# Transposing bf16 pairs as 4-byte elements in a fused attention and maxout FFN kernel, with PSUM copies re-split and the issue order redone

## The chip, the cores and the metric

One core of one Trainium2 chip runs the whole program. The metric is device time in microseconds (us), median of several executions. "Span" is the time from the first to the last instruction in a trace; it is some 1.8 us shorter than the device time. PE is TensorE (PEld its weight loads), DVE is VectorE, ACT is ScalarE, POOL is GpSimd. PSUM is the memory into which this kernel's matmuls write and from which its copies on DVE or ACT (L153, L155) read. "Clock" is the TensorE clock that was granted, as a share of full speed. Unless a run is called slow, only fast runs are compared.

## The reference, cut to what matters

```python
# q, k, v: [8, 8, 576, 64]   phi: [8, 8, 576, 32]
a = softmax(phi, axis=2)                       # over the sequence
k_m = einsum('bhsm,bhsd->bhmd', a, k)          # 32 memory slots per head
v_m = einsum('bhsm,bhsd->bhmd', a, v)
attn = softmax(q @ k_m^T / 8, axis=-1)         # over the 32 slots
x = (attn @ v_m), heads side by side           # [4608, 512]
out = max(x @ w1, x @ w2, x @ w3) @ w_out
```

A remark on what "correct" means here. The scores are so small that the output hardly depends on q: with q set to zero the reference moves by 8e-7 of its norm. The comparison with the reference passes all kernels below, even one that reads wrong q on purpose (e8_step16), so it does not prove that the new layout is right. I checked the layout by separate arithmetic: transpose 32x32 blocks of pairs, contract even and odd columns in turn, compare with q times k_m. It agreed to 1e-14. That the chip moves the pairs as intended is shown by no run, since none of them can tell.

## The kernel before

Batch by batch, letters name pieces of work that a long text puts into an order. Each engine executes its share in that order (e10 below shows DVE idle for 2.33 us with ready work behind). The pieces that matter:

```python
accp = tile_pool(bufs=4, PSUM)     # four accumulators, shared by ALL matmul groups
EVAC = {"D": "aaaa", "T": "avvva"} # who copies block n out of PSUM: a = ACT, v = DVE

# B: att_kv: k_m, v_m (PE)     N: att_kv_norm (DVE): rden, kvn; kvn holds k_m in two halves
    in0=kvp[:, g, 0:D].rearrange("p (h d) -> p h d", h=2)...   # half h = columns 32h..32h+31
# K: att_kv_t: 3 PE transposes of kvn, one DVE copy -> kvt
# Q: att_q (two halves of the heads), 32x32 blocks on DVE
    qT = work.tile([P, NP, NC, 2, R], BF16)                    # R = 32
    nc.vector.transpose(out=qT[:, j]..., in_=q[:, j]...)       # 1152 bf16 per partition
# S: att_score: 32 matmuls of 32 x 288, contraction over half h
    rhs=qT[r, j, :, h, :], start=(h == 0), stop=(h == 1)
# M, R, X: softmax over the slots (PE sums, ACT ln and exp, DVE multiply)
# D0..D3: fold v_m into w1-w3, w2-w3 and w3*w_out (PE), copied out by EVAC["D"]
# F0..F11: first FFN product; even n: relu on ACT, odd n: max on DVE
# T0..T4: output tile, 8 matmuls of 512 columns, copied out by EVAC["T"], stored
# L0, L1, L2: load phi, k and v, q of a batch   Z: warm-up matmuls without use
for w in """ E@0 Z26@0 B@0 N@0 ... B@1 N@1 D3@0 K@1
    D2@1 L1@2 D0@1 Q0@1 Q1@1 T1@0 D1@1 S@1 T3@0 M0@1 ... """.split(): ...   # piece@batch
```

The softmax here doesn't subtract the row's maximum and nothing guards it: scores larger than these inputs give would overflow.

Of the kernel before, what the change touches and what calls it, by code (L numbers as in the profile page):

```python
# [8 lines left out]
FP32 = mybir.dt.float32  # L9
BF16 = mybir.dt.bfloat16  # L10
# [5 lines left out]
def kernel(  # L16
# [14 lines left out]
    B, H, S, D = q.shape  # L31
    M = phi.shape[-1]
    P = 128
    NP = H // 2
    NG = NP // 2
    HP = P // 2
    NC = S // HP
    R = 32
# [8 lines left out]
    work = ctx.enter_context(tc.tile_pool(name="work", bufs=2))  # L47
# [24 lines left out]
    loaded = {}  # L72
# [69 lines left out]
            )  # L142


    EVAC = {"D": "aaaa", "T": "avvva"}

    def evacuate(kind, n, out_, in_):
        e = EVAC[kind][n]
        if e == "s":
            nc.scalar.copy(out=out_[:, 0], in_=in_[:, 0])  # L150
            nc.vector.tensor_copy(out=out_[:, 1], in_=in_[:, 1])
        elif e == "a":
            nc.scalar.copy(out=out_, in_=in_)  # L153
        else:
            nc.vector.tensor_copy(out=out_, in_=in_)  # L155
# [69 lines left out]
    def att_kv_norm(b):  # L225

        s = st[b]
        kvp = s["kvp"]
        rden = work.tile([P, NG], FP32, name="rden")
        nc.vector.reciprocal(out=rden, in_=kvp[:, :, 2 * D])  # L230
        kvn = work.tile([P, 3, P], BF16, name="kvn")
        nc.vector.tensor_tensor(
            out=kvn[:, 0].rearrange("p (a d) -> p a d", a=NG),
            in0=kvp[:, :, D : 2 * D],
            in1=rden.unsqueeze(2).to_broadcast([P, NG, D]),
            op=ALU.mult,
        )
        for g in range(NG):
            kn = kvn[:, 1:3, HP * g : HP * (g + 1)]
            nc.vector.tensor_scalar_mul(  # L240
                out=kn.rearrange("p h (t d) -> p h t d", t=2),
                in0=kvp[:, g, 0:D]
                .rearrange("p (h d) -> p h d", h=2)
                .unsqueeze(2)
                .to_broadcast([P, 2, 2, R]),
                scalar1=rden[:, g : g + 1],
            )
        s["kvn"] = kvn
# [12 lines left out]
    def att_q(b, n):  # L261


        s = st.setdefault(b, {})
        if "qT" not in s:
            s["qT"] = work.tile([P, NP, NC, 2, R], BF16, name="qT")
        j = halves[n]
        nc.vector.transpose(  # L268
            out=s["qT"][:, j].rearrange("p j c h r -> p (j c h r)"),
            in_=loaded[b]["q"][:, j].rearrange("p j c d -> p (j c d)"),  # L270
        )

    attns = {}
# [1 line left out]
    def att_score(b):  # L275

        s = st[b]
        kvt, qT = s["kvt"], s["qT"]
        e2 = s["e2"] = work.tile([P, NG, S], BF16, name="e2")
        if b % 2 == 0:  # L280
            attns[b // 2] = work.tile([P, NG, 2 * S], BF16, name="attn")
        sc = [
            acc_pool.tile([P, 2, BANK], FP32, name="sc", tag="acc") for _ in range(NG)
        ]
        for h in range(2):
            for j in range(NP):
                for a in range(NG):
                    for t in range(2):
                        r = slice(R * (2 * a + t), R * (2 * a + t + 1))
                        nc.tensor.matmul(  # L290
                            sc[a][M * j : M * (j + 1), t, 0:SH],
                            lhsT=kvt[r, 1 + h, M * j : M * (j + 1)],
                            rhs=qT[r, j, :, h, :],
                            start=(h == 0),
                            stop=(h == 1),
                            tile_position=(R * (2 * a + t), M * j),
                        )
        for a in range(NG):
            nc.scalar.activation(  # L299
                out=e2[:, a].rearrange("p (t r c) -> p t r c", t=2, c=NC),  # L300
                in_=sc[a][:, :, 0:SH].rearrange("p t (c r) -> p t r c", c=NC),
                func=AF.Exp,
                scale=0.125,
            )
# [96 lines left out]
    def ffn2(b, t, last=False):  # L401


        hT, attn = hts[b // 2], attns[b // 2]
        c0 = S - HP if t == 4 else (b % 2) * (S + HP) + t * P
        if last:
            return ffn2_last(b, c0)
        po = acc_pool.tile([P, DM], FP32, name="po", tag="acc")
        for fc in range(FT):
            nc.tensor.matmul(  # L410
                po,
                lhsT=hT[:, fc, c0 : c0 + P],
                rhs=wo_sb[:, fc, :],
                start=(fc == 0),
                stop=False,
            )
        for g in range(NG):
            if t < 4:
                nc.tensor.matmul(  # L419
                    po,  # L420
                    lhsT=attn[:, g, c0 : c0 + P],
                    rhs=wp3s[b][:, g, :],
                    start=False,
                    stop=(g == NG - 1),
                )
            else:
                for u in range(2):
                    nc.tensor.matmul(  # L428
                        po[HP * u : HP * (u + 1)],
                        lhsT=attn[:, g, c0 + HP * u : c0 + HP * (u + 1)],  # L430
                        rhs=wp3s[b - 1 + u][:, g, :],
                        start=False,
                        stop=(g == NG - 1),
                        tile_position=(0, HP * u),
                    )
        ot = opool.tile([P, DM], FP32, name="ot")
        r0 = (b // 2) * 2 * S + c0
        rows = out[r0 : r0 + P, :]
        evacuate("T", t, ot, po)
        nc.sync.dma_start(out=rows, in_=ot)  # L440
# [40 lines left out]
    def issue(b, n):  # L481

        if not 0 <= b < B or (n == "T4" and b % 2 == 0):
            return
        i = int(n[1:]) if len(n) > 1 else None
        {
            "L": lambda: (load_ph, load_kv, load_q)[i](b),
            "E": lambda: [att_exp(b, h) for h in (halves if b == 0 else [slice(0, NP)])],
            "B": lambda: att_kv(b) if b else first_kv(),
            "N": lambda: att_kv_norm(b),  # L490
            "K": lambda: att_kv_t(b),
            "Q": lambda: att_q(b, i),
            "S": lambda: att_score(b),
            "M": lambda: att_sum(b, i),
            "R": lambda: att_rec(b, i),
            "X": lambda: att_mul(b, i),
            "D": lambda: fold(b, i),
            "F": lambda: ffn1(b, i),
            "T": lambda: ffn2(b, i),
            "W": lambda: w3_t(i),  # L500
            "O": lambda: w3_o(i),
            "V": lambda: w_diff(i),
            "Z": lambda: warm_up(i),
        }[n[0]]()

    def run(b, text):

        for w in text.split():
            issue(b + w.count("+") - w.count("-"), w.rstrip("+-"))

    for w in """
        E@0 Z26@0 B@0 N@0 Z5@0 K@0 Q0@0 Q1@0 Z15@0 S@0 Z6@0 M1@0 R1@0 W2@0 W0@0 W1@0 M0@0
        X1@0 Z4@0 O0@0 O1@0 V0@0 R0@0 X0@0 O2@0 Z3@0 D0@0 V1@0 O3@0 F2@0 F6@0 V2@0 L2@2 F0@0
        D1@0 F4@0 D2@0 F3@0 E@1 F1@0 F10@0 F7@0 L0@2 F11@0 F8@0 F9@0 F5@0 B@1 N@1 D3@0 K@1
        D2@1 L1@2 D0@1 Q0@1 Q1@1 T1@0 D1@1 S@1 T3@0 M0@1 L0@3 Q0@2 M1@1 R0@1 R1@1 X0@1 X1@1
        E@2 T0@0 T2@0 F8@1 Q1@2 F6@1 F7@1 F2@1 L2@3 F3@1 F9@1 F4@1 D3@1 B@2 F10@1 N@2 F5@1
        F0@1 K@2 E@3 F1@1 F11@1 Q1@3 S@2 T0@1 Q0@3 M0@2 R0@2 X0@2 M1@2 L1@3 L0@4 T4@1 R1@2
        L2@4 L1@4 T3@1 L0@5 X1@2 D0@2 D2@2 B@3 D1@2 N@3 T2@1 F2@2 K@3 F10@2 F3@2 F0@2 Q0@4
        S@3 F11@2 F8@2 F4@2 F1@2 M1@3 F9@2 R1@3 E@4 F5@2 Q1@4 M0@3 R0@3 T1@1 F6@2 F7@2 D3@2
        B@4 X1@3 D2@3 D0@3 T0@2 N@4 L0@6 X0@3 K@4 L2@5 F2@3 D1@3 S@4 T1@2 E@5 F3@3 F8@3 L1@5  # L520
        F9@3 F6@3 F4@3 F10@3 L0@7 M1@4 F5@3 E@6 T2@2 R1@4 M0@4 F0@3 Q1@5 R0@4 F7@3 T3@2 L1@6
        F1@3 L2@6 F11@3 D3@3 B@5 N@5 D0@4 D1@4 T0@3 X1@4 L1@7 K@5 T1@3 D3@4 Q0@5 D2@4 X0@4
        L2@7
    """.split():
        n, b = w.split("@")
        issue(int(b), n)
    for b in range(4, B - 1):
        run(b, "T4- D3+ S+ L2++++ T3- F2 F4 Q1++ F5 F10 F3 F0 F6 F1 F8 M1+ F11 F9")
        run(b, "L0+++++ F7 R1+ M0+ X1+ T2- R0+ D2+ B++ Q0++ D1+ N++ D0+ L1++++ T1 E+++")
        run(b, "K++ X0+ T0")  # L530
    run(B - 1, "F2 F10 F6 F3 F11 F0 T2- F1 F4 F8 F9 F7 F5 T3- T4 T4- T3 T2 T1")
    ffn2(B - 1, 0, last=True)


# [28 lines left out]
```

## Time and profile before

| | before |
|---|---|
| median of the first measurement | 173.88 us (173.47 to 174.13, 4 runs) |
| span of the trace | 171.7 us |
| PE, DVE, ACT busy | 161.2, 102.4, 107.5 us |
| batch 0's first fold starts; batch 1's kv matmuls start; PE ends | 27.45; 37.50; 168.0 us |
| gaps on PE after the first fold starts | 3.76 us |

The last row is the sum of the seven bracketed idle times that PE's timeline lists after its first fold (the prediction below shows them). That list leaves out idle times of some 0.1 us. It is the number to follow through this document.

The groups that the change touches, from the view of groups by shape. Columns: line, engine, operation, output and inputs, shapes, count; busy us and mean ns of one; idle before them and what ended it.

```profile
L153 ACT CAST wp<-wps 128x1024 bf16<-128x1024 f32 x32 | 31.3, 1017 | 10.3 <-PE wps L355 10.2
L268 DVE STREAM_TRANSPOSE qT<-qq 128x1152 bf16<-128x1152 bf16 x16 | 21.6, 1364 | 1.7 <-DMA qq<-in_q_dram 1.7
L155 DVE COPY ot<-po 128x512 f32<-128x512 f32 x24 | 16.6, 690 | 30.5 <-PE po L419 30.5
L153 ACT COPY ot<-po 128x512 f32<-128x512 f32 x11 | 6.4, 584 | 11.4 <-PE po L428 6.3 <-PE po L419 4.8
L290 PE MATMUL sc<-qT,kvt 32*32 32x288 bf16 x256 | 3.7, 286 | 0.0
```

The transposes take 21.6 us of DVE, a fifth of its busy time; all fold copies are on ACT.

### The profile page before, as it was taken

How to read it: one execution, taken by the hardware profiler on the slowest of the kernel's cores; microseconds unless marked ns; L12 is line 12 of the kernel's file. 1: busy time of each engine (PE TensorE's matmuls, PEld its weight loads, DVE VectorE, ACT ScalarE, POOL GpSimd, SP SyncE). 2: the span in 40 equal slices, each digit the busy share in tenths (PEclk: the TensorE clock that was granted, in tenths of full speed). 3: DMA queues.
4: the chain of work that ended last, by engine and by line, in shares of the span. 5: the costliest groups of instructions: out<-in, count | busy, mean ns of one | idle time of the engine just before them, and what ended most of it. 6: DMA issues, size and time to landing. Idle time of an engine off the chain costs nothing.

```text
span 171.7 us, 4491 instructions
## 1 busy us (share of the span) xinstructions
PE 161.2 (94%) x1925; PEld 91.5 (53%) x1948; DVE 102.4 (60%) x160; ACT 107.5 (63%) x154; POOL 28.3 (17%) x43
## 2 busy tenths in 40 slices
PE   7999999987999999899999997999999999999991
PEld 2354644552567546664755445654764475466350
DVE  6407346679588945795468546883787058337240
ACT  4100528946897877899996586886785777752100
POOL 7951111110515100051332110000000000000000
PEclk9999999999999999999999999999999999999998
DMA  5999999999999999999999999953103310221333
GB/s 157 162 202 211 206 211 274 211 207 266 222 314 262 216 298 260 237 244 258 230 247 290 232 258 244 224 131 124 65 0 107 141 65 4 112 75 61 119 126 124
DMA packets 21973, 31.76 MB, mean 185 GB/s; under 512 B 1216, under 2 KB 16576, under 8 KB 21952
## 3 DMA queue, kind: packets, MB, share of 16 engines
q0 software_dynamic: 16080, 21.43, 65.3%
q1 hardware_dynamic: 5728, 9.90, 16.5%
q8 instruction: 15, 0.25, 0.6%
q10 hardware_dynamic: 144, 0.13, 0.2%
q14 instruction: 6, 0.05, 0.1%
HBM read 39.32 MB, written 9.44 MB: 284 GB/s over the span
## 4 chain that ended last, share of the span: by engine, by line
PE 43%; DMA 41%; issue 6%; DVE 3%; POOL 3%; ACT 1%; POOLq 0%
DMA kvo<-in_v_dram 20%; PE po L410 16%; PE acc L380 15%; DMA ph<-in_phi_dram 11%; DMA qq<-in_q_dram 10%; PE po L419 5%; POOL kvo L96 3%; PE wps L355 2%; PE kvp L216 2%; DVE qT L268 2%; PE sm L311 1%; PE po L451 1%; PE po L428 1%; ACT e L205 1%; PE sc L290 0%
## 5 line engine op out<-in xcount | busy, mean ns | idle before, releaser
L380 PE MATMUL acc<-attn,wp 128*128 128x288 bf16 x384 | 51.2, 286 | 1.3 <-DVE hT L392 1.0
L410 PE MATMUL po<-wo_sb,hT 128*128 128x512 bf16 x191 | 50.1, 379 | 1.1
L380 PEld LDWEIGHTS <-wp 128*128 128x128 bf16 x384 | 37.0, 98 | 13.8 <-issue 1.9
L392 DVE TENSOR_TENSOR hT<-acc,h 128x576 bf16<-128x576 f32 x48 | 34.4, 749 | 12.6 <-PE acc L380 8.3
L153 ACT CAST wp<-wps 128x1024 bf16<-128x1024 f32 x32 | 31.3, 1017 | 10.3 <-PE wps L355 10.2
L390 ACT ACTIVATE h<-acc 128x576 bf16<-128x576 f32 x48 | 29.8, 652 | 11.2 <-PE acc L380 9.9
L155 DVE COPY ot<-po 128x512 f32<-128x512 f32 x24 | 16.6, 690 | 30.5 <-PE po L419 30.5
L410 PEld LDWEIGHTS <-hT 128*128 128x128 bf16 x210 | 19.4, 98 | 23.2 <-issue 4.4
L268 DVE STREAM_TRANSPOSE qT<-qq 128x1152 bf16<-128x1152 bf16 x16 | 21.6, 1364 | 1.7 <-DMA qq<-in_q_dram 1.7
L140 PE MATMUL po<-warm 128*128 128x512 bf16 x65 | 18.2, 428 | 1.5 <-DVE warm L128 1.2
L419 PE MATMUL po<-wp,attn 128*128 128x512 bf16 x62 | 18.4, 379 | 0.0
L299 ACT ACTIVATE e<-sc 128x576 bf16<-128x576 f32 x16 | 9.6, 661 | 10.7 <-PE sc L290 10.7
L153 ACT COPY ot<-po 128x512 f32<-128x512 f32 x11 | 6.4, 584 | 11.4 <-PE po L428 6.3
L335 DVE TENSOR_TENSOR attn<-e,r 128x576 bf16<-128x576 bf16 x16 | 11.9, 746 | 1.0 <-ACT r L330 1.0
L140 PEld LDWEIGHTS <-warm 128*128 128x128 bf16 x68 | 6.9, 108 | 10.3 <-issue 4.0
L205 ACT ACTIVATE e<-ph 128x1152 bf16<-128x1152 f32 (+1 forms) x9 | 9.6, 1064 | 4.5 <-DMA ph<-in_phi_dram 4.5
L324 ACT ACTIVATE ln<-sm 128x576 f32<-128x576 f32 x16 | 10.4, 649 | 1.7 <-PE sm L311 1.6
L89 POOL DMA_DIRECT2D ph<-in_phi_dram x7 | 5.3, 756 | 36.9 <-ACT e L205 33.4
L330 ACT ACTIVATE r<-ln 128x576 f32<-128x576 f32 x16 | 10.9, 683 | 0.5
L419 PEld LDWEIGHTS <-attn 128*128 128x128 bf16 x62 | 6.1, 98 | 7.3
L216 PE MATMUL kvp<-kvo,e 64*32 64x192 bf16 x576 | 8.3, 243 | 0.8 <-DMA kvo<-in_v_dram 0.8
L355 PE MATMUL wps<-w_sb,kvt 64*32 64x512 bf16 x192 | 8.3, 381 | 0.9 <-DVE kvt L258 0.5
(45 smaller groups left out, 100.8 us busy)
## 6 DMA issues: line engine op xcount, KB each, us to landing
out_dram<-ot SPq DMA_DIRECT2D x35, 256.0 KB, 4.1
qq<-in_q_dram POOLq DMA_DIRECT2D x8, 576.0 KB, 16.2
ph<-in_phi_dram POOLq DMA_DIRECT2D x7, 576.0 KB, 17.9
kvo<-in_k_dram POOLq DMA_DIRECT2D x7, 576.0 KB, 16.3
kvo<-in_v_dram POOLq DMA_DIRECT2D x7, 576.0 KB, 18.5
w_sb<-in_moe_w_dram POOLq DMA_DIRECT2D x3, 768.0 KB, 19.0
wo_sb<-in_moe_w_out_dram POOLq DMA_DIRECT2D x1, 768.0 KB, 16.7
ph<-in_phi_dram SPq DMA_DIRECT2D x2, 288.0 KB, 4.4
```

The source lines that it names most:

```text
L140: nc.tensor.matmul(po[:, 0:BANK], lhsT=warm[:, 0:P], rhs=warm, start=True, stop=True)
L153: nc.scalar.copy(out=out_, in_=in_)
L155: nc.vector.tensor_copy(out=out_, in_=in_)
L216: nc.tensor.matmul(kvp[M * j : M * (j + 1), a, 0 : 3 * D], lhsT=s["e"][r, j, c, :], rhs=kv[r, :, j, c, :], start=(c == 0), stop=(c == NC - 1),
L268: nc.vector.transpose(out=s["qT"][:, j].rearrange("p j c h r -> p (j c h r)"), in_=loaded[b]["q"][:, j].rearrange("p j c d -> p (j c d)"),)
L335: nc.vector.tensor_tensor(out=attns[b // 2][:, g, (b % 2) * S : (b % 2 + 1) * S], in0=s["e2"][:, g, 0:S], in1=s["r", g], op=ALU.mult,)
L355: nc.tensor.matmul(ps[M * j : M * (j + 1), a, :], lhsT=s["kvt"][r, 0, M * j : M * (j + 1)], rhs=w12[r, j, n * BANK : (n + 1) * BANK] if n ...
L380: nc.tensor.matmul(acc[:, h, 0:SH], lhsT=wps[b][:, g, w * DF + ft * P : w * DF + (ft + 1) * P], rhs=attn[:, g, c0 : c0 + SH], start=(g == ...
L390: nc.scalar.activation(out=h1, in_=a, func=AF.Relu)
L392: nc.vector.tensor_tensor(out=hT[:, ft, (b % 2) * S : (b % 2 + 1) * S].rearrange("p (h n) -> p h n", h=2), in0=a, in1=s["h1", ft], op=ALU.max,
L410: nc.tensor.matmul(po, lhsT=hT[:, fc, c0 : c0 + P], rhs=wo_sb[:, fc, :], start=(fc == 0), stop=False,)
L419: nc.tensor.matmul(po, lhsT=attn[:, g, c0 : c0 + P], rhs=wp3s[b][:, g, :], start=False, stop=(g == NG - 1),)
```

## The change

The intent: two neighbouring bf16 are to travel through the 32x32 transpose as one 4-byte element, which halves the count (576 per partition instead of 1152). That the two then arrive unchanged and side by side is assumed; as said above, no run shows it. On that assumption the score contraction no longer runs over columns 0 to 31 and then 32 to 63, but over even columns and then odd ones. k_m is split the same way. DVE's saved time takes over some PSUM copies from ACT, and the issue order is redone for these durations.

```diff
-    EVAC = {"D": "aaaa", "T": "avvva"}
+    EVAC = {"D": "avaa", "T": "vavav"}
...
-                .rearrange("p (h d) -> p h d", h=2)
+                .rearrange("p (d h) -> p h d", h=2)
...
-            s["qT"] = work.tile([P, NP, NC, 2, R], BF16, name="qT")
+            s["qT"] = work.tile([P, NP, NC, R, 2], BF16, name="qT")
...
-            out=s["qT"][:, j].rearrange("p j c h r -> p (j c h r)"),
-            in_=loaded[b]["q"][:, j].rearrange("p j c d -> p (j c d)"),
+            out=s["qT"][:, j].rearrange("p j c r e -> p (j c r e)").bitcast(FP32),
+            in_=loaded[b]["q"][:, j].rearrange("p j c d -> p (j c d)").bitcast(FP32),
...
-                            rhs=qT[r, j, :, h, :],
+                            rhs=qT[r, j, :, :, h],
...  (the order text, cut to the start of batch 1)
-  ... B@1 N@1 D3@0 K@1 D2@1 L1@2 D0@1 Q0@1 Q1@1 T1@0 D1@1 S@1 T3@0 ...
+  ... B@1 N@1 Q0@1 T3@0 K@1 Q1@1 T1@0 S@1 D1@1 L2@2 D0@1 ...
```

More of the change, by code (lines that the diff above doesn't have):

```diff
@@ L511 @@
     for w in """
-        E@0 Z26@0 B@0 N@0 Z5@0 K@0 Q0@0 Q1@0 Z15@0 S@0 Z6@0 M1@0 R1@0 W2@0 W0@0 W1@0 M0@0
-        X1@0 Z4@0 O0@0 O1@0 V0@0 R0@0 X0@0 O2@0 Z3@0 D0@0 V1@0 O3@0 F2@0 F6@0 V2@0 L2@2 F0@0
-        D1@0 F4@0 D2@0 F3@0 E@1 F1@0 F10@0 F7@0 L0@2 F11@0 F8@0 F9@0 F5@0 B@1 N@1 D3@0 K@1
-        D2@1 L1@2 D0@1 Q0@1 Q1@1 T1@0 D1@1 S@1 T3@0 M0@1 L0@3 Q0@2 M1@1 R0@1 R1@1 X0@1 X1@1
-        E@2 T0@0 T2@0 F8@1 Q1@2 F6@1 F7@1 F2@1 L2@3 F3@1 F9@1 F4@1 D3@1 B@2 F10@1 N@2 F5@1
-        F0@1 K@2 E@3 F1@1 F11@1 Q1@3 S@2 T0@1 Q0@3 M0@2 R0@2 X0@2 M1@2 L1@3 L0@4 T4@1 R1@2
-        L2@4 L1@4 T3@1 L0@5 X1@2 D0@2 D2@2 B@3 D1@2 N@3 T2@1 F2@2 K@3 F10@2 F3@2 F0@2 Q0@4
-        S@3 F11@2 F8@2 F4@2 F1@2 M1@3 F9@2 R1@3 E@4 F5@2 Q1@4 M0@3 R0@3 T1@1 F6@2 F7@2 D3@2
-        B@4 X1@3 D2@3 D0@3 T0@2 N@4 L0@6 X0@3 K@4 L2@5 F2@3 D1@3 S@4 T1@2 E@5 F3@3 F8@3 L1@5
-        F9@3 F6@3 F4@3 F10@3 L0@7 M1@4 F5@3 E@6 T2@2 R1@4 M0@4 F0@3 Q1@5 R0@4 F7@3 T3@2 L1@6
-        F1@3 L2@6 F11@3 D3@3 B@5 N@5 D0@4 D1@4 T0@3 X1@4 L1@7 K@5 T1@3 D3@4 Q0@5 D2@4 X0@4
-        L2@7
+        E@0 Z26@0 B@0 N@0 Z5@0 K@0 Q0@0 Q1@0 Z8@0 S@0 Z8@0 W1@0 W2@0 M0@0 W0@0 L0@2 R0@0
+        Z9@0 O2@0 M1@0 V0@0 X0@0 R1@0 O0@0 X1@0 V2@0 O3@0 L1@2 Z3@0 D0@0 O1@0 F6@0 F0@0 F2@0
+        D2@0 F4@0 V1@0 D3@0 D1@0 F7@0 F5@0 F10@0 F11@0 F1@0 E@1 F3@0 F8@0 F9@0 B@1 N@1 Q0@1
+        T3@0 K@1 Q1@1 T1@0 S@1 D1@1 L2@2 D0@1 M0@1 M1@1 R1@1 R0@1 X1@1 T0@0 X0@1 T2@0 E@2
+        D3@1 F2@1 F0@1 F3@1 D2@1 B@2 N@2 F1@1 Q1@2 F8@1 Q0@2 L0@3 F6@1 F4@1 L1@3 F10@1 K@2
+        F7@1 F5@1 L2@3 S@2 F11@1 D2@2 F9@1 E@3 M0@2 T2@1 M1@2 R0@2 R1@2 X0@2 L0@4 T0@1 D0@2
+        X1@2 D3@2 B@3 N@3 D1@2 L1@4 T1@1 F2@2 F6@2 Q1@3 F3@2 E@4 K@3 F8@2 L2@4 F7@2 L0@6
+        Q0@3 F4@2 F10@2 F5@2 F0@2 S@3 L0@5 T4@1 M1@3 F11@2 R1@3 F1@2 M0@3 R0@3 X0@3 T3@1
+        F9@2 D2@3 D1@3 L2@5 X1@3 B@4 D0@3 T1@2 F8@3 L1@5 N@4 F2@3 K@4 F9@3 Q1@4 F10@3 F0@3
+        E@5 F3@3 Q0@4 F4@3 T3@2 S@4 F5@3 F1@3 L1@6 T0@2 F6@3 M0@4 M1@4 F11@3 R0@4 T2@2 R1@4
+        F7@3 D3@3 B@5 D3@4 Q0@5 Q1@5 D2@4 L2@6 N@5 X1@4 T0@3 L1@7 X0@4 K@5 T1@3 L2@7 D0@4
+        D1@4 E@6 L0@7
     """.split():
@@ L527 @@
     for b in range(4, B - 1):
-        run(b, "T4- D3+ S+ L2++++ T3- F2 F4 Q1++ F5 F10 F3 F0 F6 F1 F8 M1+ F11 F9")
-        run(b, "L0+++++ F7 R1+ M0+ X1+ T2- R0+ D2+ B++ Q0++ D1+ N++ D0+ L1++++ T1 E+++")
-        run(b, "K++ X0+ T0")
-    run(B - 1, "F2 F10 F6 F3 F11 F0 T2- F1 F4 F8 F9 F7 F5 T3- T4 T4- T3 T2 T1")
-    ffn2(B - 1, 0, last=True)
+        run(b, "L0+++++ D1+ T4- S+ T3- F6 F2 F0 F4 F7 F3 Q0++ F8 F10 F1 M1+ F11 F9 Q1++")
+        run(b, "M0+ R1+ R0+ X1+ F5 T2- D0+ B++ D3+ L2++++ D2+ T1 L1++++ N++ K++ E+++ X0+")
+        run(b, "T0")
+    run(B - 1, "F4 F6 F2 F0 F5 T2- F8 F7 F1 F3 F9 F10 T4- F11 T3- T4 T1 T2 T0")
+    ffn2(B - 1, 3, last=True)
 _INS = ['q', 'k', 'v', 'phi', 'moe_w1', 'moe_w2', 'moe_w3', 'moe_w_out']
```

## The prediction

> **What bounds the kernel now.** I read the summary of busy times first, then the table of stretches, then PE's timeline for its gaps, then DVE's timeline for what ended the largest of them. The busy times of the page before:
>
> ```profile
> PE 161.2 (94%) x1925; PEld 91.5 (53%) x1948; DVE 102.4 (60%) x160; ACT 107.5 (63%) x154; POOL 28.3 (17%) x43
> ```
>
> PE is taken 94% of 171.7 us; DVE and ACT, between which this change shifts work, only 60% and 63%. A busy PE is not by itself a PE at its peak, so I checked its pace: in the chain of waits 12 matmuls of 288 columns of L380 take 1.47 us, 122.5 ns each, or 2.35 columns per ns, and no stretch of that kind goes faster. PE streams at its full pace nearly everywhere. Next, where it does not; the columns are the stretch, its length, then PE, PEld, DVE, ACT and POOL busy (us), clock, DMA share and GB/s:
>
> ```profile
> 18.00:37.00 19.00, 17.86 (x168) 10.03 (x169) 10.47 (x15) 13.26 (x20) 3.73 (x5) 1.00 1.18 224
> 37.00:41.00 4.00, 2.35 (x100) 1.32 (x101) 2.82 (x8) 1.22 (x2) 0.00 (x0) 1.00 1.21 209
> 41.00:110.00 69.00, 66.85 (x923) 39.66 (x932) 47.48 (x73) 56.12 (x80) 14.16 (x19) 1.00 1.14 256
> 110.00:168.00 58.00, 57.51 (x609) 33.11 (x616) 33.05 (x53) 33.92 (x49) 0.00 (x0) 1.00 0.28 90
> 168.00:171.70 3.70, 0.01 (x1) 0.00 (x0) 0.00 (x0) 0.37 (x1) 0.00 (x0) 0.82 0.37 130
> ```
>
> From 110 to 168 us PE idles 0.49 us in 58: nothing to win. The tail of 3.7 us (last copy, last store) stays as it is. PE idles 1.65 us between 37 and 41, 2.15 between 41 and 110, 1.14 between 18 and 37. Before that it mostly runs warm-up matmuls that wait for data (18.2 us of them in all). So about 5 us of idle PE can be touched. Its gaps, from PE's timeline; the bracket has the idle time and what ended it:
>
> ```profile
> 27.45 0.41 PE L355 MATMUL wps<-w_sb,kvt 64*32 64x512 bf16 x8 [0.30 <-DVE w_sb L188]
> ...
> 32.48 4.19 PE L380 MATMUL acc<-attn,wp 128*128 128x288 bf16 x32 [0.29 <-ACT wp L153]
> 37.50 0.94 PE L216 MATMUL kvp<-kvo,e 64*32 64x192 bf16 x72 [0.83 <-DMA kvo<-in_v_dram]
> ...
> 39.06 0.23 PE L256 MATMUL kvtp<-ident,kvn 128*128 128x128 bf16 x1 [0.41 <-DVE kvn L232]
> 39.58 0.28 PE L256 MATMUL kvtp<-ident,kvn 128*128 128x128 bf16 x2 [0.29 <-DVE kvn L240]
> 40.31 0.63 PE L355 MATMUL wps<-w_sb,kvt 64*32 64x512 bf16 x16 [0.45 <-DVE kvt L258]
> ...
> 71.68 0.41 PE L311 MATMUL sm<-e,blkones 128*128 128x288 bf16 x2 [0.52 <-DVE hT L392]
> ...
> 106.39 1.63 PE L380 MATMUL acc<-attn,wp 128*128 128x288 bf16 x12 [0.97 <-DVE hT L392]
> ```
>
> And what kept DVE before the last of these, from DVE's timeline:
>
> ```profile
> 104.32 1.38 DVE L268 STREAM_TRANSPOSE qT<-qq 128x1152 bf16<-128x1152 bf16 x1 [1.11 <-DMA qq<-in_q_dram]
> 105.62 1.39 DVE L392 TENSOR_TENSOR hT<-acc,h 128x576 bf16<-128x576 f32 x2
> ```
>
> DVE runs in order: a transpose stood waiting 1.11 us for its q, then ran 1.38, and the max that would empty the FFN's accumulators stood behind it. The transfers are the second limit: their share is over 1.1 until 110 us, so a load that is placed later lands later.
>
> [...] The trace has one size: 1152 elements in 1364 ns, [...] but nothing yet shows that 4-byte elements go at the same rate per element. [...] The new score operand takes every second bf16[...]; no matmul of the kernel before reads that way. [...] savings on DVE count only where they close one of these gaps.
>
> **The change, part by part.**
> Transposes: 16 of 1152 elements become 16 of 576. [...] 16 x 0.60 = 9.6 us less DVE time.
> Fold copies: the second of the four per batch moves from ACT to DVE, 8 in all. ACT loses 8 x 1.017 (L153) = 8.1 us. DVE gains 8 times [...] 1.22 us, = 9.8 us.
> Output copies: the pattern "avvva" becomes "vavav". In the new order 20 whole ones stand on DVE instead of 24: DVE -4 x 0.69 = -2.8 us, ACT +4 x 0.584 = +2.3 us.
> Sums: DVE 102.4 - 9.6 + 9.8 - 2.8 = 99.8 us; ACT 107.5 - 8.1 + 2.3 = 101.7 us. Both were off the bound and stay off it. PE's instructions are the same in number and shape (1925 seen; 68 warm-ups issued in both), so its work stays.
> The strided read of kvp by the 16 kvn operations (342 ns each) I take as free.
> Issue order, which is where the time must come from:
> (a) Start. The first fold waits for a subtraction whose w1 lands at 26.17 us; that load's place in the queue is unchanged. In both orders the attention of batch 0 is done about then, so D0 still starts near 27.4. A faster transpose at 15 us only means fewer warm-ups before the scores. Nothing gained.
> (b) 27 to 37 us. D3 of batch 0 now goes before batch 1's kv matmuls, which wait until 37.4 for v of batch 1 in any case; that fills a hole, -0.34 us. Against it: the column block D1 now comes after D2 and D3 and is emptied by DVE (1.22 against 1.02), with six maxes of 0.75 behind it. By hand that puts PE at batch 1's kv matmuls at about 37.2, just in time.
> (c) 37 to 41. The 0.41, 0.29 and 0.45 us gaps are the chain kv, norm, transpose, copy, with nothing beside it. The new order puts a whole output tile T3 (8 x 0.215 = 1.72 us) between norm (0.17 + 0.29 + 0.60 us) and transpose, and T1 before the scores: -1.15 us.
> (d) 41 to 110. q of batch 6 is loaded before the last phi, not after (576 KB, about 3 us at 0.2 KB/ns), and its transpose moves behind more of the maxes: the 0.97 us gap should close. The 0.52 at 71.7 has a transpose of 1.38 in front of the max as well (69.61), now 0.76: it probably closes.
> Sum: 0.34 + 1.15 + 0.97 + 0.52 = 3.0 us. A new order of a program that has four accumulators and waits in order also makes new gaps; I take 1.2 us for them, a judgement (the old order had 2.15 us in 69). Net -1.8 us: 174.1 - 1.8 = **172.3 us**.
>
> **Rivals.**
> R1: DVE's 9.6 us come off the end in full, 164.5 us. Against it: DVE is 60% busy and PE has only about 5 us of gaps. I rule it out.
> R2: a 4-byte transpose takes as long as two 2-byte ones. Then DVE stands at 109.4 us, still under PE, but each fold copy on DVE delays maxes and transposes by 1.2 us with nothing given back. I would expect the gains of (d) to be lost: 173.5 to 175 us. Chance about 12%.
> R3: PE reads every second bf16 at half rate. 256 score matmuls, eight bursts of 0.40 us each (the chain of waits), would double: +3.2 us, 175.5 us. [...] chance 4%.
> R4: the transfers set the pace up to 110 us, so order does not matter there: only (b) and (c) count, 172.6 less new gaps, about 173.3 us. It shares much with my own theory: the 0.83 us at 37.5 is such a wait and stays.
>
> **Range and chances.** All five touchable gaps closed and none new would be 171.1 us, and "faster by over 2%" needs 170.6, so it needs more than I can find: 8%. Slower by over 2% is 177.6 us and needs R3 together with R2 or a bad order: 3%. The rest is within 2%. Eight in ten: 171.0 to 174.2 us.
>
> **What would show it.** Transposes of 128x576 4-byte elements near 0.76 us (R2: 1.3). Score bursts still 0.40 us. Eight fold copies on DVE near 1.2 us; DVE busy near 100, ACT near 102, PE within 1 us of 161 less closed gaps. First fold near 27.4 and batch 1's kv matmuls at 37.4 to 37.6, behind the same transfer; scores of batch 1 near 41.8 instead of 43.0, without a wait for DVE. No gap near 1 us behind a transpose that waits for q. From 110 us to PE's end at most 0.6 us of gaps. I am wrong if the first fold or the kv matmuls of batch 1 move by over 1 us, which would mean that the transfers of the start depend on the order after all, or if new gaps exceed 2 us, above all DVE's max behind fold copies.

## The result, and the profile after

The changed kernel took 171.44 us (171.11 to 172.3, 4 runs) against 173.88, ratio 0.987 (95% interval 0.9825 to 0.9914). A second measurement, run e0_after below, gave 171.0 us and 0.9845. A ratio here is the mean time of one kernel's fast runs over that of the other's of the same rounds, so it is not quite the ratio of the medians. The gain is 1.3 to 1.6%, inside the 2% band.

Busy times of the page after, to hold against those of before in the prediction:

```profile
PE 161.3 (95%) x1927; PEld 91.1 (54%) x1948; DVE 98.9 (58%) x164; ACT 101.3 (60%) x150; POOL 28.4 (17%) x43
```

PE's busy time is the same to 0.1 us. DVE and ACT lost 3.5 and 6.2 us, but they were not the bound. The groups, by shape:

```profile
L153 ACT CAST wp<-wps 128x1024 bf16<-128x1024 f32 x24 | 23.6, 1016 | 5.4 <-PE wps L355 5.3
L155 DVE COPY ot<-po 128x512 f32<-128x512 f32 x20 | 13.8, 688 | 17.8 <-PE po L419 12.5 <-PE po L428 5.1
L268 DVE STREAM_TRANSPOSE qT<-qq 128x576 f32<-128x576 f32 x16 | 12.0, 762 | 0.8 <-DMA qq<-in_q_dram 0.8
L155 DVE CAST wp<-wps 128x1024 bf16<-128x1024 f32 x8 | 9.7, 1218 | 2.1 <-PE wps L355 2.1
L290 PE MATMUL sc<-qT,kvt 32*32 32x288 bf16 x256 | 4.0, 294 | 0.0
```

A transpose went from 1364 to 762 ns, a fold copy costs DVE 1218 ns where it cost ACT 1017, and a score matmul takes 294 ns against 286. The last stretches of the table of stretches (stretch, length, PE, PEld, DVE, ACT, POOL busy, clock, DMA share, GB/s), cut at PE's new end:

```profile
37.00:41.00 4.00, 3.41 (x87) 2.04 (x87) 2.68 (x7) 0.85 (x2) 1.98 (x3) 1.00 1.15 281
41.00:110.00 69.00, 68.19 (x1026) 40.09 (x1034) 48.48 (x81) 53.28 (x80) 12.69 (x17) 1.00 1.17 254
110.00:165.60 55.60, 55.03 (x528) 31.57 (x521) 29.44 (x49) 31.02 (x47) 0.00 (x0) 1.00 0.24 90
```

PE's idle time fell from 1.65 to 0.59 us between 37 and 41, and from 2.15 to 0.81 between 41 and 110; the late part was full before and is full now. (Both traces lack some 20 of PE's 1948 matmul records, and a lost record looks like idle time in this table; the listed gaps are the firmer measure.) What is left as gaps on PE after the first fold, from PE's timeline:

```profile
31.05 0.41 PE L355 MATMUL wps<-w_sb,kvt 64*32 64x512 bf16 x8 [0.43 <-DVE w_sb L188]
...
34.06 3.10 PE L380 MATMUL acc<-attn,wp 128*128 128x288 bf16 x24 [0.26 <-ACT wp L153]
37.70 0.94 PE L216 MATMUL kvp<-kvo,e 64*32 64x192 bf16 x72 [0.54 <-DMA kvo<-in_v_dram]
```

With one of 0.16 us near the end that is 1.39 us, against 3.76. **The gaps shrank by 2.37 us, and the time by 2.4 us.** The rest of the stretch from first fold to PE's end is 138.31 - 1.39 = 136.9 us after and 140.56 - 3.76 = 136.8 us before: the work is unchanged.

The agreement to 0.1 us is closer than the measure allows. The second trace of the change, e0_after, has this line in place of the last one above:

```profile
37.95 0.94 PE L216 MATMUL kvp<-kvo,e 64*32 64x192 bf16 x72 [0.96 <-DMA kvo<-in_v_dram]
```

Its gaps are 1.66 us, so 2.10 closed, and its span is 169.6 us, again 2.1 shorter; but its rest is 165.91 - 27.16 - 1.66 = 137.1 us. The split is good to some 0.3 us.

### The profile page after: what moved, and what is told of

It reads as the page before. It is cut to its first block, busy times and chain, and to the rows that moved or that the text cites. A ratio compares the mean times of both kernels' runs of the same rounds, so it can differ in the third digit from the quotient of the medians.

```text
span 169.3 us, 4498 instructions
## 1 busy us (share of the span) xinstructions
PE 161.3 (95%) x1927; PEld 91.1 (54%) x1948; DVE 98.9 (58%) x164; ACT 101.3 (60%) x150; POOL 28.4 (17%) x43
## 4 chain that ended last, share of the span: by engine, by line
PE 74%; DMA 20%; issue 1%; POOL 1%; ACT 1%; POOLq 0%
PE po L410 27%; PE acc L380 25%; DMA kvo<-in_v_dram 20%; PE po L419 8%; PE wps L355 4%; PE kvp L216 3%; PE sm L311 2%; PE sc L290 1%; POOL kvo L96 1%; PE po L428 1%; PE po L451 1%; PE kvtp L256 1%; ACT e L299 1%; ACT ot L153 0%; PE po L459 0%
## 5 line engine op out<-in xcount | busy, mean ns | idle before, releaser
L380 PE MATMUL acc<-attn,wp 128*128 128x288 bf16 x384 | 52.0, 286 | 0.3 <-ACT wp L153 0.3
L390 ACT ACTIVATE h<-acc 128x576 bf16<-128x576 f32 x48 | 28.6, 654 | 11.3 <-PE acc L380 11.3
L153 ACT CAST wp<-wps 128x1024 bf16<-128x1024 f32 x24 | 23.6, 1016 | 5.4 <-PE wps L355 5.3
L155 DVE COPY ot<-po 128x512 f32<-128x512 f32 x20 | 13.8, 688 | 17.8 <-PE po L419 12.5
L140 PE MATMUL po<-warm 128*128 128x512 bf16 x65 | 17.7, 420 | 1.5 <-DVE warm L128 1.2
L153 ACT COPY ot<-po 128x512 f32<-128x512 f32 x15 | 8.8, 588 | 16.0 <-PE po L419 16.0
L268 DVE STREAM_TRANSPOSE qT<-qq 128x576 f32<-128x576 f32 x16 | 12.0, 762 | 0.8 <-DMA qq<-in_q_dram 0.8
L155 DVE CAST wp<-wps 128x1024 bf16<-128x1024 f32 x8 | 9.7, 1218 | 2.1 <-PE wps L355 2.1
L96 POOL DMA_DIRECT2D kvo<-in_k_dram x9 | 6.8, 750 | 20.7 <-PE wps L355 13.0
```

What stands on the lines that cost most here:

```text
L140: nc.tensor.matmul(po[:, 0:BANK], lhsT=warm[:, 0:P], rhs=warm, start=True, stop=True)
L153: nc.scalar.copy(out=out_, in_=in_)
L155: nc.vector.tensor_copy(out=out_, in_=in_)
L268: nc.vector.transpose(out=s["qT"][:, j].rearrange("p j c r e -> p (j c r e)").bitcast(FP32), in_=loaded[b]["q"][:, j].rearrange("p j c d - ...
L380: nc.tensor.matmul(acc[:, h, 0:SH], lhsT=wps[b][:, g, w * DF + ft * P : w * DF + (ft + 1) * P], rhs=attn[:, g, c0 : c0 + SH], start=(g == ...
L390: nc.scalar.activation(out=h1, in_=a, func=AF.Relu)
```

## The experiments

All ran beside the kernel before; "gaps" is the sum of PE's listed gaps after the first fold in the profiled run. Two theories were set against each other. **G**: PE is the bound, and only gaps closed on PE count. **W**: the work taken from DVE and ACT counts by itself.

| run | median us | ratio to before | DVE busy | gaps us |
|---|---|---|---|---|
| before | 173.5 | 1 | 102.4 | 3.76 |
| the change, e0_after | 171.0 | 0.985 | 99.0 | 1.7 |
| e1_only_transpose | 172.28 | 0.993 | 93.6 | 2.16 |
| e2_no_transpose, e2b | 176.99 | 1.020 | 108.0 | 5.48 |
| e3_old_copies | 179.27 | 1.034 | 91.8 | 7.80 |
| e4_only_copies | 178.76 | 1.031 | 108.2 | 5.90 and clock |
| e5_bare_chain | 176.41 | 1.019 | 99.0 | 4.22 and clock |
| e6_phi_first | 170.83 | 0.986 | 98.9 | 0.70 |
| e7_only_q_early | 172.56 | 0.994 | no usable trace | - |
| e8_step16 (one look) | 175.55 | - | 98.9 | 0.77 |
| e9_bare_chain_warm | 174.32 | 1.004 | 99.1 | 1.47 |
| e10_old_output_copies | 176.95 | 1.019 | 101.2 | 5.78 |

At 2% only e3 and e4 are clearly slower than the kernel before; e2, e5 and e10 lie above it with their whole interval but are "unclear" at 2%. Differences between two rows are taken from medians, partly of different rounds. The new order alone, with old transposes and old copies, was not run.

### e0_after: the change once more

No edit.

> The changed kernel itself, as the measure for the runs beside it. 171.4 us, ratio 0.985 to 0.989 to the kernel before.

Measured 171.0 us (170.48 to 171.73), ratio 0.9845 (0.9818 to 0.9872). It repeats, and it is the measure for the kernels made from the change.

### e1_only_transpose: the 4-byte transposes alone

The kernel before with the changed lines of kvn, qT, the transpose and the score operand; old copies, old order.

> The kernel before with the 4-byte transposes alone (and the layout they need); old order, old copies. Theory G (only closed gaps of PE count): of PE's gaps the 0.52 us at 71.7 closes and the 0.97 us at 106 shrinks by the 0.60 us that a transpose gets shorter, so about 1.0 us faster: 172.9 us. Theory W (DVE's and ACT's busy time counts): DVE falls to 92.8 us, less than the 98.9 of the full change, so this should be as fast as the full change or faster: 171.4 us or less.

Measured 172.28 us, ratio 0.9928: 1.3 us faster than before, 1.3 slower than the full change. DVE has its second lowest load of all runs here (93.6 us) and still the full change is faster with 99. W fails. The gaps of 0.52 and 0.97 us are both gone from PE's timeline; the second was expected to shrink only. DVE's timeline shows why:

```profile
103.44 0.78 DVE L268 STREAM_TRANSPOSE qT<-qq 128x576 f32<-128x576 f32 x1 [0.73 <-DMA qq<-in_q_dram]
104.15 1.38 DVE L392 TENSOR_TENSOR hT<-acc,h 128x576 bf16<-128x576 f32 x2
```

DVE still waits for q here (0.73 us instead of 1.11). But the max behind the transpose begins 0.71 us after the transpose starts instead of 1.30, and begins 1.47 us earlier than in the kernel before (104.15 against 105.62); PE no longer waits for it.

### e2_no_transpose and e2b_no_transpose_again: the change without the 4-byte transposes

Order and copies new, the five transposing lines old.

> The changed kernel with 2-byte transposes (order and copies new). Theory G: the scores of batch 1 stand behind two transposes of 1.36 us each, which begin when q lands at 40.5, so they start near 43.6 instead of 42.3 and PE gets a gap of about 1.3 us there; most other transposes have slack. About 172.7 us. Theory W: DVE rises to 108.5 us, above the kernel before: 174 us or more.

> The same kernel as e2_no_transpose, whose only trace fell in a slow run, for a trace of a fast one: 176.9 us. Its fast runs had a granted clock of 1.00, so the 5.9 us that it loses to the changed kernel must be gaps of PE. Theory G: they stand before the scores of several batches (PE waits for a transpose) and behind maxes that stand in DVE's queue after a transpose, over 5 us in sum. Theory W: no such gaps, but slower operations.

Measured 176.99 us, ratio 1.0197. The profiled execution of the first run was slow (clock 0.66, 240 us), so the same kernel was run once more for a trace: 176.94 us, clock 1.00 (a single run, so its state is unknown, but its time is that of the fast ones). My expectation of 172.7 was far off: I had looked at batch 1 alone. W's "174 or more" was nearer in the number, but its reason is not what the trace shows. PE's waits in that trace (who waited for whom, us in total, times, longest):

```profile
PE sc L290 <- DVE qT L268: 2.5, 4, 0.9
...
PE kvtp L256 <- DVE kvn L240: 1.0, 1, 1.0
PE sc L290 <- DVE kvt L258: 0.9, 1, 0.9
```

Scores of several batches wait for their transposes or for a copy behind one, and the norm of one batch stands behind two transposes. Taking off the 5.48 us of listed gaps leaves 138.3 us of the stretch from first fold to PE's end, 1.4 more than in the change. The table of stretches has it as PE's busy time: 136.98 us against 135.64 there, with nearly the same number of records. So 4.1 us of the 5.9 that this kernel loses to the change are named gaps. The rest may be stops too: a matmul of 288 columns is listed with 286 ns, but in an unbroken stream the next one starts after 122.5, so a listed gap can understate a stop by some 0.16 us, and there are 9 gaps more here (an estimate: 1.5 us; not tested, and the kernel before, with 3 gaps more than the change, shows no such excess).

### e3_old_copies and e10_old_output_copies: the change with copies split as before

```diff
-    EVAC = {"D": "avaa", "T": "vavav"}
+    EVAC = {"D": "aaaa", "T": "avvva"}    # e3
+    EVAC = {"D": "avaa", "T": "avvva"}    # e10
```

> The changed kernel with the copies split as in the kernel before (fold copies all on ACT). Theory G: the new order counts on the split as on the transposes; each relu of the FFN that stands behind a fold copy on ACT comes 1.0 us later, and PE waits for accumulators: 172 to 174 us. Theory W: DVE falls to 92, ACT rises to 107, sum unchanged: 171.4 us.

> The changed kernel with only the output copies split as before (fold copies as in the change). Theory G: a copy of output tile T1 then stands on DVE ahead of the norm of the next batch, and PE waits 1.2 + 0.3 us before the transposes of each late batch, as in the trace of e3_old_copies at 118 and 136 us; with less loss elsewhere than there: 175 to 178 us. Rival: the fold copies made the loss of e3_old_copies; then 171 to 172 us.

e3: 179.27 us, ratio 1.0337, the slowest of all, with the lowest DVE load (91.8 us). W fails again, and my range for G (172 to 174) was much too narrow. e10: 176.95 us, ratio 1.019, inside the range expected. So the old split of the output copies alone cost about 5.9 us and that of the fold copies about 2.3 more. Of the 5.9, 4.1 are listed gaps (5.78 against 1.66 in e0_after); PE's busy time from first fold to end is longer by the rest (138.39 against 136.71), as in e2b. In e3's trace PE waits for fold copies on ACT for 1.17 us at 34.69 (0.26 in the change), 0.50 at 45.19 and 1.14 at 103.30, which is the size of the other 2.3. e10's timeline of DVE and PE near 116 us:

```profile
114.90 0.69 DVE L155 COPY ot<-po 128x512 f32<-128x512 f32 x1 [2.33 <-PE po L419]
115.51 0.16 DVE L230 RECIPROCAL rden<-kvp 128x2 f32<-128x2 f32 x1
...
116.05 0.23 PE L256 MATMUL kvtp<-ident,kvn 128*128 128x128 bf16 x1 [1.19 <-DVE kvn L232]
...
116.57 0.28 PE L256 MATMUL kvtp<-ident,kvn 128*128 128x128 bf16 x2 [0.29 <-DVE kvn L240]
```

DVE sits idle for 2.33 us because the next thing in its order is the copy of an output tile that PE has not finished. The norm of the next batch, whose data are ready, stands behind that copy; then PE waits 1.19 and 0.29 us for the norm. It recurs at 134 us: from 110 us to PE's end PE idles 2.96 us, twice 1.48. DVE is not busy here, it is blocked. With "vavav" that tile is copied by ACT, which has room (busy for 99.2 us of 171.7 up to PE's end).

### e4_only_copies: the new copy split alone

The kernel before with the new EVAC line.

> The kernel before with the new split of the PSUM copies alone. Theory G: no gap of PE is closed and DVE has 7 us more in front of its maxes: 174.0 to 175.5 us. Theory W: DVE 109, ACT 102: sum of both is about the same, so 174 us.

Measured 178.76 us, ratio 1.0313, 3 us beyond what I expected of G. The gaps are 5.90 us, but the trace has a granted clock of 0.981 as well, while most kernels here have 0.99 to 1.00. Cut into single microseconds, the clock falls to 0.50 for about three of them at 40 us and again at 85, each time after PE had idled for most of a microsecond or two (1.08 us between 38 and 40, 1.88 between 81 and 84). The clock lost in the two drops sums to 3.4 us; with 2.1 of added gaps that is 5.6 of the 6.9 us by which the stretch from first fold to PE's end grew. That was not in any theory of mine, and e5 and e9 look into it.

### e5_bare_chain and e9_bare_chain_warm: nothing beside the chain; then fillers beside it

```diff
-  ... B@1 N@1 Q0@1 T3@0 K@1 Q1@1 T1@0 S@1 D1@1 ...        # the change
+  ... B@1 N@1 Q0@1 K@1 Q1@1 S@1 T3@0 T1@0 D1@1 ...        # e5
+  ... B@1 N@1 Q0@1 Z5@1 K@1 Z9@1 Q1@1 S@1 T3@0 T1@0 D1@1  # e9: 14 useless matmuls
```

> The changed kernel with the two output tiles of batch 0 put behind the scores of batch 1, not between norm, transpose and scores. Theory G: the gaps of the kernel before at 38 to 41 us come back (0.41, 0.29) and the scores wait for q, which lands at 40.5, and for two transposes: about 2 us of gaps in all, 172.5 to 173.5 us, more if the clock drops after them as in e4_only_copies. Rival T (transfers set the pace to 110 us): the work is only moved in time, 171.4 us.

> e5_bare_chain with 14 idle matmuls put into its gaps at 38 to 42 us (5 before the transposes of batch 1, 9 between them and the scores; 3 us of PE in all). They do nothing useful and fill time in which PE waits anyway. If the drop of the clock to 0.5 that followed these gaps in e5_bare_chain comes from PE's idling, it goes away and the time falls by 1.2 to 2 us from 176.4, to 174.5 to 175.2 us, with a granted clock near 1.0. If the drop has another cause, 176.4 us or more.

e5: 176.41 us, ratio 1.019; e9: 174.32 us, ratio 1.004. e5 lost 5.4 us to the change, more than the 1 to 2 expected. e9 fell just under its expected range of 174.5 to 175.2. The work was not simply moved in time (rival T). Its table of stretches (columns as above; PE busy third, clock third from the end):

```profile
38.00:39.00 1.00, 0.37 (x33) 0.20 (x12) 0.96 (x4) 0.00 (x0) 0.38 (x1) 1.00 1.12 353
39.00:40.00 1.00, 0.42 (x3) 0.11 (x2) 0.41 (x3) 0.00 (x0) 1.00 (x2) 1.00 1.07 336
40.00:41.00 1.00, 0.00 (x0) 0.00 (x0) 1.00 (x3) 0.00 (x0) 0.09 (x1) 1.00 1.25 248
41.00:42.00 1.00, 0.61 (x32) 0.29 (x32) 0.66 (x1) 0.00 (x0) 0.04 (x1) 0.65 1.13 194
42.00:43.00 1.00, 0.93 (x25) 0.28 (x3) 0.00 (x0) 0.55 (x2) 0.70 (x1) 0.50 1.21 203
43.00:44.00 1.00, 0.85 (x2) 0.30 (x2) 0.00 (x0) 0.64 (x2) 0.00 (x0) 0.50 1.23 211
44.00:45.00 1.00, 1.00 (x4) 0.40 (x3) 0.00 (x0) 0.00 (x0) 0.00 (x0) 0.65 1.22 210
```

PE is busy for 0.79 us of the 3 from 38 to 41, in pieces, with no single listed gap above 1.32 us; then the clock drops to half. The lost clock is 0.35 + 0.50 + 0.50 + 0.35 = 1.7 us. Gaps beyond those of the change (4.22 - 1.39 = 2.8) and 1.7 make 4.5 us; PE ends 4.3 us later (169.98 against 165.65). This trace is of the fastest of the six runs (175.44 us, clock 0.99); three others had clock 0.977 and took 176.85 to 177.62 us, and where they lost it was not traced.

In e9 fillers take the idle time, and the clock stays:

```profile
40.00:41.00 1.00, 1.00 (x8) 0.48 (x7) 0.25 (x2) 0.00 (x0) 0.96 (x2) 1.00 1.14 262
41.00:42.00 1.00, 1.00 (x7) 0.46 (x5) 1.00 (x3) 0.00 (x0) 0.00 (x0) 1.00 1.23 240
42.00:43.00 1.00, 1.00 (x35) 0.31 (x33) 0.69 (x2) 0.00 (x0) 0.01 (x1) 1.00 1.16 197
```

Useless work made the kernel 2.1 us faster by the medians (2.7 by the two ratios): the drop comes from PE's idling, since that alone was taken away. Against the change e9 still loses 3.3 us, which is about what its 14 fillers occupy (39.09 to 40.18 and 40.42 to 42.45 us in its timeline, 3.1 us). So putting T3 and T1 beside the chain, as the change does, is worth the gap and the insurance against the clock. Here a sum of 2.2 us of idle in 3 us was enough for a drop to 0.50. Where the line lies is not shown: the kernel before idles 1.66 us between 36 and 40 us and keeps its clock, e4 idles 1.94 us in the same four and drops to 0.50.

### e6_phi_first and e7_only_q_early: the order of the last loads

e6 is the change with phi loaded in the order of the batches and the last phi ahead of q of batch 6. e7 is the kernel before with the last phi moved to the end.

```diff
-  ... F10@3 L0@7 M1@4 ... D2@4 X0@4 L2@7          # before
+  ... F10@3 M1@4 ... D2@4 X0@4 L2@7 L0@7          # e7
-  ... F7@2 L0@6 Q0@3 ... S@3 L0@5 T4@1 ... D2@4 L2@6 ... E@6 L0@7     # the change
+  ... F7@2 L0@5 Q0@3 ... S@3 L0@6 T4@1 ... D2@4 L0@7 L2@6 ... E@6     # e6
```

> The changed kernel with phi loaded in the order of the batches and the last phi ahead of q of batch 6, as in the kernel before. If that load order is part of the gain also here, q of batch 6 lands about 3 us later, DVE waits for it with maxes behind it, and PE gets a gap near 105 us of up to 1 us: 171.5 to 172.3 us. If the shorter transposes and the new order have made it unimportant, 171.2 us, same as the change.

> The kernel before with one change: the last phi is loaded last, so q of batch 6 lands about 3 us earlier. Theory G: the 0.97 us gap at 106 closes: 172.6 us. Rival: the gap is DVE's own lateness and not the transfer's: 173.6 us.

e7: 172.56 us (five fast runs, 172.01 to 173.14), ratio 0.9944: in the old kernel the earlier q is worth about 1.0 us (0.5 to 1.5 by the interval 0.9915 to 0.9973), the size of the gap it was meant to close. Its profiled execution took 580 us with a recorded clock of 1.0, PE's first 26 warm-up matmuls in 21.39 us against 8.42 in the kernel before, but DVE and ACT busy for only 105.6 and 112.0 us in all, so that PE alone was slow; that trace is not used, and the gap itself was not seen to close. e6: 170.83 us, ratio 0.9857 (0.9824 to 0.9891), the same as the change: there this load order makes no difference that can be seen. The transpose of batch 6 starts at 104.17 us without waiting, behind two maxes:

```profile
102.83 1.42 DVE L392 TENSOR_TENSOR hT<-acc,h 128x576 bf16<-128x576 f32 x2 [3.94 <-PE acc L380]
104.17 0.77 DVE L268 STREAM_TRANSPOSE qT<-qq 128x576 f32<-128x576 f32 x1
```

### e8_step16: the disputed read, made worse

```diff
-    rhs=qT[r, j, :, :, h],
+    rhs=qT[r].rearrange("p j c (r8 s) e -> p (j c r8) (s e)", s=4)[:, :, h],
```

The result is wrong on purpose (and passes the comparison all the same, see above).

> The changed kernel with the score operand read at every eighth bf16 (16 bytes apart[...]) instead of every second; the result is wrong on purpose, the number and size of matmuls is the same. [...] each burst of 32 score matmuls takes about twice as long, 0.8 us instead of 0.41[...]. Rival: PE reads any step at full rate, the burst stays at 0.41.

One look: 175.55 us (a single run, its state unknown). The group of score matmuls:

```profile
L290 PE MATMUL sc<-qT,kvt 32*32 32x288 bf16 x256 | 9.9, 673 | 0.1
```

In PE's timeline a burst of 32 starts at 41.77 us and the next matmul behind it at 42.93: 1.16 us, against 0.41 in the change (42.29 to 42.70).

```profile
41.77 1.23 PE L290 MATMUL sc<-qT,kvt 32*32 32x288 bf16 x32
42.93 0.63 PE L355 MATMUL wps<-w_sb,kvt 64*32 64x512 bf16 x16
```

A step of 16 bytes costs 2.8 times (1.16 us a burst against 0.41), more than the double that I expected. The first of the eight bursts stands before the first fold, where PE waits for weights anyway (first fold at 27.41); the other seven take 8.15 us from start to next start, against 3.16 in the change, 5.0 more. With 0.6 us fewer gaps that gives the 4.4 us by which PE ends later (170.08 against 165.65). The change's step of 4 bytes costs 8 ns a matmul in the mean (294 against 286) and nothing measurable per burst (0.41 us, against 0.40 in the chain of waits of the kernel before).

No version beat the change clearly; e6 is equal to it.

## Why the prediction was right

**The bound.** PE's work from first fold to its end is 136.8 us before and 136.9 after; the gain is its closed gaps (2.37 us; 2.10 in e0_after's trace) to within some 0.3 us. e1 and e3, with the least DVE load, refute the rival that counts work (R1). R4, that order does not matter before 110 us because transfers set the pace, fails as well: the gaps of 0.52 and 0.97 us there closed, and e7 gained 1.0 us by the order of the loads alone.

**The parts.** The 0.60 us that a transpose would save and the 1.22 us of a fold copy on DVE were estimates of mine that no trace had shown when I made them; measured are 1364 - 762 = 602 ns and 1.218 us. The strided read of kvp, taken as free, was free: a kvn operation (L240) takes 341 ns against 342. DVE was estimated at 99.8 us, measured 98.9; ACT at 101.7, measured 101.3. Rival R2 (4-byte elements at half rate) is gone: 576 of them take 762 ns where 1152 of 2 bytes take 1364, so moving bf16 in pairs saves 44%. R3 (half-rate strided reads) is gone too: 0.41 us a burst. That PE would read every second bf16 without loss was my expectation, shown by no run before.

**(a) and (b), the start.** First fold at 27.34 us, as said. PE was ready for batch 1's kv matmuls at 37.16 (34.06 + 3.10), expected 37.2; but v of batch 1 landed at 37.70, not 37.4, so the 0.83 us gap only shrank to 0.54. And (b) overlooked a gap: 0.43 us at 31.05, where a fold waits for a subtraction on DVE that began at 29.78, when its weights had landed. So between 28 and 38 us the gaps did not fall by 0.34 but rose by 0.11 us (0.29 + 0.83 before, 0.43 + 0.26 + 0.54 after). When v lands also differs from one execution to the next: the kv matmuls start at 37.70 here, at 37.95 in e0_after after 0.96 us of waiting, and at 37.13 without any in e6, whose order up to there is the same. The spans of these last two traces differ by the same 0.8 us (169.6 and 168.8).

**(c), the chain.** The three gaps (1.15 us) closed. The scores of batch 1 started at 42.29 where I said 41.8: 0.2 is the later v, the rest my sum of the pieces, which dropped the transposes of batch 1 and the starts between pieces. I did not know that the place was also the edge of a clock drop (e5, e9).

**(d), the two gaps near 72 and 106.** Both closed. In the kernel before, loads issued one behind another at 84.2 (phi), 84.9 (k), 85.8 (v) and 86.6 us (q of batch 6) landed in that order, at 93.0, 97.0, 99.9 and 104.3; in the change that q was issued at 84.0 and landed at 100.7. The reason I gave for the second, q being loaded earlier, seems enough by itself in the old kernel (e7, 1.0 us by its time) but is not what does it in the new one: e6 takes it back without loss, and e1 closes the gap by shorter transposes alone. The causes overlap; I credited one.

**The term that was mis-sized** is the allowance of 1.2 us for new gaps. Two are new, 0.43 us at 31.05 and 0.16 near the end, 0.59 in all. What closed comes to 1.15 + 0.97 + 0.52 and 0.32 at the start (0.29 + 0.83 became 0.26 + 0.54), 2.96 us where 3.0 was said. So the 0.6 us by which 1.8 fell short of 2.4 is this allowance. It was a judgement and not a calculation, and that it came so near is partly luck: the same kind of estimate missed e2, e3 and e5 by 3 to 5 us.

**What I would have got wrong** without the experiments is how tightly the order is bound to the durations. Hand estimates from one place gave 172.7 for e2, 172 to 174 for e3, about 173 for e5; measured were 177.0, 179.3 and 176.4. The order that gains 2.4 us with 762 ns transposes loses 3.4 against the kernel before with 1364 ns ones. Why a single copy moved between engines costs so much was seen in e10: the norm of a batch queues behind a copy that has to wait.

## What to carry to other kernels

Where one engine is the bound and the rest have room, a saving elsewhere was worth the gaps of the bound that it closed, to some 0.3 us here; list these gaps, with what ended each, before and after. On engines that work in order, ask not only how long an operation takes but what stands ready behind it while it waits: DVE at 58% blocked PE at 93% in e10. Durations, copy split and issue order are one design: the transposes alone were worth -1.3 us here, the copy split alone +5.2, of which some 3.4 are lost clock, all three together -2.4 to -2.6.
